# One scan-attention and two-MLP kernel on one Trainium2 core: squared products copied out of PSUM by one ScalarE operation, the last attention outputs in the state's bank, and fp32 key-value products in the first attention

## The chip, the cores and the metric

The kernel runs on 1 core of one Trainium2 chip. The metric is the device time of one execution in microseconds (us). The kernel before takes 816.45 us (median of 3 runs, 816.13 to 817.19). PE is TensorE, DVE is VectorE, ACT is ScalarE, POOL is GpSimd, and SP is the engine whose queue issues every DMA here.

## What is computed

There are three stages for each of four batch entries (S = 768 positions, H = 8 heads, D = 48, C = H*D = 384).

```python
# 1. attention with a decaying complex state, position by position
S_re, S_im = ar * S_re - ai * S_im + outer(k[t], v[t]), ar * S_im + ai * S_re
y[t] = q[t] @ S_re
# 2. token mixing, then channel mixing (256 and 1536 hidden)
u = x + (relu(x.T @ w_tok1) @ w_tok2).T
x = u + relu(u @ w_ch1) @ w_ch2
# 3. a gated layer with squared relu (1024 hidden) on a mix of each row and the row before
out = sigmoid(xr @ w_r) * (relu(xk @ w_k) ** 2 @ w_v)
```

## The kernel before, in words

**Attention.** The scan is done in 6 blocks of 128 positions (J = 0 to 5). Decays and angles are first turned into logs and summed (the words S, L, A, R, C, D of `SEQ0` and `SEQ1`), and then one step per block follows (T0 to T7, since later parts of a block's work come one or two steps after its first). `ORD0` and `ORD1` (L35, L36) give the order of the parts within a step by hand; the digit behind a name says how many blocks back it works. The parts are: `b` scales q and k by their decays (DVE); `q` and `k` turn them into complex pairs `q2`, `k2` in fp32 (DVE, tile `Wc`) and take the upper fp16 part (ACT); `e` takes the lower fp16 part (DVE); each of these four fp16 parts is transposed by a DMA (`transposed`, L546). `w` splits v into the fp16 parts `vh` (ACT) and `vl` (DVE). `f` makes the scores (PE, 12 products per group of four heads) and `m` masks them (DVE). `u` (L624) makes k x v for the state: 24 fp16 products of 128 x 48, three for each head, plus two with an identity matrix that add the state carried over. `v` takes the state out of its PSUM bank as two fp16 parts (ACT, then DVE). `h` (L668) makes the outputs y in PSUM from the transposed q, the state and the masked scores, and `i` takes them out as `xh` (ACT) and `xl` (DVE). `l` loads q, k and v two blocks on.

In the first attention (b = 0) nothing of another batch entry runs beside it. There the scores times v are fp32 products, with a scaled fp32 copy `v32` of v that the part `a` (L558) makes at the end of a step. Its banks alternate between two pairs. In it, PE's, ACT's and DVE's instructions of the steps are chained in the order of `ORD0` (L334 to L346 and L479 to L483), and every load and transpose is chained in SP's queue (`queue`, L524). For blocks below 3, `keep_busy` (L485) adds 6 idle products (fillers, tile `h1b`, L489) behind each part that issues products; they have the lowest priority. In the other attentions (b = 1 to 3) there is one bank "u" for the state and one bank "y" for the outputs.

**Dense layers.** `dense(b)` runs beside `attention(b + 1)`; the main loop (L960 to L974) advances the two in proportion to costs written by hand. `two_layers` (L796) goes through items (t, f). For each item it makes 9 products into one of two PSUM banks (`ps_d`, tile `ps`), and `evac1` takes the result out as two fp16 parts in the tile `g`. The second layer's 9 products on these parts come `LAG` = 2 items later. For the gated layer (wk1 and wv2, 16 items for each batch entry) `wk1_out` (L907) does three ACT operations and one DVE operation on the bank:

```python
ACT(ps, ps, ACTF.Relu)                                   # L908
ACT(ps, ps, ACTF.Square, scale=...)                      # L909
ACT(part[:, 0], ps, ACTF.Copy)                           # L910
last_ev[:] = [TT(part[:, 1], ps, part[:, 0], op=SUB)]    # L911
```

Weights arrive as pairs of 32-bit words and are unpacked on DVE (L266 to L268), rounded to the upper fp16 part (DVE L271 or ACT L273) and to the lower one (DVE L277); they load into two buffers `wst`. A small ACT operation `seen` (L186) collects sums of squares for a validity test at the end, one column of the tile `low` for each call. The program is ordered before it runs: each instruction has a priority, and the order on each engine comes from these priorities and from the chains.

Of the kernel before, what the change touches and what calls it, by code (L numbers as in the profile page):

```python
# [8 lines left out]
F32 = mybir.dt.float32  # L9
# [4 lines left out]
ACTF = mybir.ActivationFunctionType  # L14
# [3 lines left out]
B, H, S, D = 4, 8, 768, 48  # L18
C = H * D
NJ = S // 128  # L20
# [11 lines left out]
SEQ0 = "S0 L0 S1 L1 B1 A0 R0 A1 R1 C0 C3 C1 C4 C2 D0 C5 D1 T0 T1 T2 T3 T4 T5 T6 T7"  # L32
SEQ1 = "S0 S1 L0 L1 A0 R0 A1 R1 C0 C1 C2 D0 C3 C4 C5 D1 T0 T1 T2 T3 T4 T5 T6 T7"

ORD0 = "f01 f11 b0 w0 q0 k0 e0 i2 v1 u0 m01 m11 h01 h11 x2 a0 l0"  # L35
ORD1 = "b0 w0 u1 v1 q0 f01 m01 g01 f11 k0 h01 m11 g11 e0 h11 i1"  # L36

BEHIND = "fh"
# [17 lines left out]
X_S, U_S, XK_S, XR_S, SQ_S = 6, 5, 5, 3, 14  # L56
T1_S, T2_S, C1_S, C2_S, WK_S, WV_S, WR_S = 6, 5, 6, 7, 6, 6, 3
# [11 lines left out]
ROUND_L = 1.5 * 2.0 ** (11 + L_S + 1)  # L69


STATS = {"wp": 8, "wm": 8, "wbits": 1, "wsum": 26, "xsum": 48, "osum": 24, "low": 36, "re": 2, "rmin": 6}
NSTAT = sum(STATS.values()) + STATS["wp"] + STATS["wm"]
LOW_MIN = 48.0
UNIT = 2.0 ** L_S
# [25 lines left out]
def split_path(  # L101
# [10 lines left out]
    MUL, ADD, SUB, MAX, MIN = ALU.mult, ALU.add, ALU.subtract, ALU.max, ALU.min  # L112
# [205 lines left out]
    def hd(x):  # L318
        return x.rearrange("p (h d) -> p h d", h=H)
# [5 lines left out]
    last_ev = []  # L325
    tables = [None, [], []]

    def attention(b):
# [75 lines left out]
        def bank(tag, J, shape):  # L404
            if b == 0 and J % 2:
                return ps_a.tile(shape, F32, tag={"u": "a0", "y": "a1"}[tag], name=tag)
            return ps_1.tile(shape, F32, tag=tag, name=tag)
# [73 lines left out]
        def MM(**k):  # L481
            last_mm[:] = [nc.tensor.matmul(**k)]  # L482
            behind(last_mm, ahead if b == 0 else passed)  # L483
# [73 lines left out]

        def s_a(J):  # L558
            d = st[J]
            d["v32"] = hd(V32[J % 2])  # L560
            ACT(d["v32"], d["v"], ACTF.Copy, scale=col_c[:, 2:3])
            if J + 1 < NJ:
                turn(J + 1)
            return 0.0

        def s_b(J):
# [9 lines left out]
                load(J + 1, "q")  # L576
            return 1.33

        def s_w(J):
            d = st[J]  # L580
            ACT(d["vh"], d["v"], ACTF.Copy, scale=col_c[:, 2:3])
            STT(d["vl"], d["v"], col_c[:, 2:3], d["vh"], op0=MUL, op1=SUB)
            if J == 0:
                seen(d["vh"][:, :, 0:LOW_N // H])
            if b > 0:
                load(J + 1, "v")
            return 0.5
# [36 lines left out]
        def s_u(J):  # L624

            if J == NJ - 1:
                return 0.0
            d = st[J]
            U = bank("u", J, [128, H, D])
            Uf = d["U"] = U.rearrange("p h d -> p (h d)")  # L630
            with tc.high_priority(offset=P_PE):
                def carried():
                    for i in range(2 if J > 0 else 0):
                        MM(out=Uf, lhsT=id1[0:96], rhs=T16[0:96, 2 * i + J % 2], start=b > 0 and i == 0, stop=b == 0 and i == 1)

                if b > 0:
                    carried()
                for h in range(H):
                    for n_, (a_, b_) in enumerate(THREE):
                        MM(out=U[:, h], lhsT=sets[J % 2]["k" + a_][:, h], rhs=d["v" + b_][:, h],  # L640
                                         start=(J == 0 or b == 0) and h == 0 and n_ == 0, stop=h == H - 1 and n_ == 2 and (b > 0 or J == 0))
                if b == 0:
                    carried()
            return 0.0
# [23 lines left out]
        def s_h(J, g):  # L668
            d = st[J]
            if g == 0:  # L670
                d["y"] = bank("y", J, [128, H, D])
            y = d["y"]
            with tc.high_priority(offset=P_PE):
                for h in range(4 * g, 4 * g + 4):
                    if J > 0:
                        th, tl = hd(T16[0:96, J % 2]), hd(T16[0:96, 2 + J % 2])
                        for n_, (a_, b_) in enumerate((("h", th), ("h", tl), ("l", th))):
                            MM(out=y[:, h], lhsT=Tr[J % 2]["q" + a_][0:96, h], rhs=b_[:, h], start=n_ == 0, stop=False)
                    if b == 0:
                        MM(out=y[:, h], lhsT=d["m", g][:, h % 4], rhs=d["v32"][:, h], start=J == 0, stop=True)  # L680
                    for n_, (m_, v_) in enumerate(((0, "vh"), (0, "vl"), (1, "vh")) if b > 0 else ()):
                        MM(out=y[:, h], lhsT=M16[g][m_][:, h % 4], rhs=d[v_][:, h], start=J == 0 and n_ == 0, stop=n_ == 2)
            return 0.0
# [22 lines left out]
            return lambda J: fn(J, *a)  # L706

        cq, ck = late(s_c, "q"), late(s_c, "k")
        fns = {"a": s_a, "x": s_x, "l": s_l, "b": s_b, "w": s_w, "q": cq, "k": ck, "e": s_e, "i": s_i, "u": s_u, "v": s_v}
        fns.update({nm + str(g): late(fn, g) for nm, fn in (("f", s_f), ("g", s_g), ("h", s_h), ("m", s_m)) for g in range(2)})  # L710
        order = [(x[0], fns[x[:-1]], int(x[-1])) for x in (ORD0 if b == 0 else ORD1).split()]

# [38 lines left out]
    def dense(b):  # L751
# [44 lines left out]
        def two_layers(nf, first, second, evac1, evac2, at=None):  # L796

            items = [(t, f) for t in range(2) for f in range(nf)]
            parts, acc = {}, {}
            for n_ in range(len(items) + LAG):  # L800
                if n_ < len(items):
                    t, f = items[n_]
                    ps = ps_d.tile([128, N], F32, tag="d", name="ps")
                    first(t, f, ps)
                    part = gring.tile([128, 2, N], F16, tag="g", name="g")
                    with tc.high_priority(offset=P_EV):
                        evac1(ps, part)
                        if n_ == 0:
                            seen(part[:, 0, 0:LOW_N])
                    parts[t, f] = part  # L810
                    yield 9 * MM
                    if at and n_ in at:
                        yield from at[n_]()
                if n_ >= LAG:
                    t, f = items[n_ - LAG]
                    if f == 0:
                        acc[t] = [ps_a.tile([128, N], F32, tag=f"a{i}", name=f"a{i}") for i in range(3)]
                    part = parts.pop((t, f))
                    for i in range(3):
                        second(t, f, i, part, acc[t][i], f == 0, f == nf - 1)  # L820
                        if f == nf - 1:
                            evac2(t, i, acc[t][i])
                    yield 9 * MM
# [8 lines left out]
            for c in range(3):  # L832
                mm3(ps, [w[:, c, 128 * f:128 * f + 128] for w in wc1], [x[:, c] for x in u[t]], c == 0, c == 2)

        def ch1_out(ps, part):
            ACT(part[:, 0], ps, ACTF.Relu)  # L836
            last_ev[:] = [STT(part[:, 1], ps, 0.0, part[:, 0], op0=MAX, op1=SUB)]  # L837

# [65 lines left out]
            for c in range(3):  # L904
                mm3(ps, [w[:, c, 128 * f:128 * f + 128] for w in wk], [x[:, c] for x in xk[t]], c == 0, c == 2)

        def wk1_out(ps, part):  # L907
            ACT(ps, ps, ACTF.Relu)  # L908
            ACT(ps, ps, ACTF.Square, scale=2.0 ** (SQ_S // 2 - XK_S - WK_S))  # L909
            ACT(part[:, 0], ps, ACTF.Copy)  # L910
            last_ev[:] = [TT(part[:, 1], ps, part[:, 0], op=SUB)]  # L911

        def wv2(t, f, jj, part, ps, start, stop):
            need(("v", f))
# [331 lines left out]
```

## Time and profile before

| what | value |
|---|---|
| median of the runs | 816.45 us |
| the profiled execution | 818.82 us, of which the span is 817.0 us |
| mean granted TensorE clock | 0.974 of full |
| PE busy | 741.3 us (91%) |
| DVE busy | 581.8 us (71%) |
| ACT busy | 522.6 us (64%) |

The profiled execution lies 2.37 us above the median, and its span is 1.82 us shorter than its own time. The first attention takes the span's first 115 us or so. dense(0) to dense(3) begin at about 116, 320, 500 and 671 us. In the rows below, a time in square brackets is the idle time of the engine before that row and what ended it.

### The profile page before, as it was taken

The page shows a single profiled execution, that of the slowest core. Times are in us where ns is not written, and L with a number is a line of the kernel's source. Part 1 is how long each engine was busy: PE and PEld are TensorE (multiplying, and loading weights), DVE is VectorE, ACT ScalarE, POOL GpSimd, SP SyncE. Part 2 cuts the span into 40 slices and gives each one's busy share as a digit, 9 for nine tenths or more (in the row PEclk, how much of TensorE's full clock was granted, in tenths as well). Part 3 has the DMA queues.
Part 4 walks back from the last instruction along what each step waited for, and adds up shares of the span by engine and source line. Part 5 has one row for each costly group of instructions (what it writes and reads, how often), then busy time and mean ns, then how long its engine had stood idle before and what let it go on. Part 6 is the DMA issues. An engine that isn't in the chain of part 4 may idle for free.

```text
span 817.0 us, 15178 instructions
## 1 busy us (share of the span) xinstructions
PE 741.3 (91%) x6107; PEld 471.4 (58%) x6107; DVE 581.8 (71%) x1016; ACT 522.6 (64%) x988; POOL 21.3 (3%) x53
## 2 busy tenths in 40 slices
PE   0968878999989889999998989999999999999996
PEld 0557845455555455555665656566666666666553
DVE  3998978999998738887768448777776454484822
ACT  7884559777588779674568778566576532142752
POOL 3000000001010000000000000000000000010000
PEclk9987989999999999999999989999999999999998
DMA  8249983444673851052336331141333342868200
GB/s 273 78 118 205 195 264 136 130 154 118 176 137 82 194 120 49 20 122 55 62 63 120 91 85 49 46 104 26 63 62 63 81 134 79 268 198 261 103 30 33
DMA packets 137949, 94.92 MB, mean 116 GB/s; under 512 B 104592, under 2 KB 120208, under 8 KB 137872
## 3 DMA queue, kind: packets, MB, share of 16 engines
q1 hardware_dynamic: 137872, 93.88, 45.2%
q8 instruction: 50, 0.82, 0.4%
q14 instruction: 27, 0.22, 0.1%
HBM read 63.97 MB, written 4.72 MB: 84 GB/s over the span
## 4 chain that ended last, share of the span: by engine, by line
PE 47%; DVE 21%; ACT 15%; DMA 12%; issue 3%; SPq 1%; DVEq 0%; ACTq 0%
PE ps L741 22%; PE a L741 14%; PE y L482 4%; DVE X L337 4%; ACT X L337 3%; DMA X<-by_time_a_re_dram 3%; PE u L482 3%; DMA wst<-in_moe_w_k_dram 2%; DVE Wc L337 2%; PE sp L482 2%; ACT tmp L875 2%; DMA Rc<-qh 1%; DVE g L837 1%; DMA wst<-in_moe_w_v_dram 1%; DVE ql L337 1%
## 5 line engine op out<-in xcount | busy, mean ns | idle before, releaser
L741 PEld LDWEIGHTS <-wc 128*128 128x128 f16 x1728 | 166.7, 98 | 116.9 <-issue 9.5
L741 PE MATMUL ps<-uh,wc 128*128 128x384 f16 x576 | 156.3, 326 | 2.1 <-DVE ul L793 1.2
L741 PE MATMUL a<-g,wc 128*128 128x384 f16 x864 | 157.9, 326 | 0.0
L741 PE MATMUL ps<-xkh,wk 128*128 128x384 f16 x384 | 106.4, 331 | 3.5 <-DVE g L911 3.3
L741 PE MATMUL a<-wv,g 128*128 128x384 f16 x576 | 106.9, 328 | 2.5 <-ACT g L910 2.5
L836 ACT ACTIVATE g<-ps 128x384 f16<-128x384 f32 x96 | 46.4, 484 | 78.0 <-PE ps L741 76.6
L741 PE MATMUL ps<-ul,wc 128*128 128x384 f16 x288 | 93.8, 326 | 0.0
L482 PEld LDWEIGHTS <-Rc 96*128 96x128 f16 (+1 forms) x1416 | 69.8, 100 | 34.4 <-issue 13.9
L837 DVE SCALAR_TENSOR_TENSOR g<-ps,g 128x384 f16<-128x384 f32 x96 | 52.9, 554 | 37.4 <-ACT g L836 37.2
L741 PEld LDWEIGHTS <-wk 128*128 128x128 f16 x576 | 55.6, 99 | 39.9 <-issue 6.4
L741 PEld LDWEIGHTS <-g 128*128 128x128 f16 x576 | 54.9, 98 | 37.4 <-ACT g L910 3.0
L741 PE MATMUL ps<-xkl,wk 128*128 128x384 f16 x192 | 63.5, 331 | 0.0
L911 DVE TENSOR_TENSOR g<-ps,g 128x384 f16<-128x384 f32 x64 | 35.3, 553 | 35.1 <-ACT g L910 34.9
L482 PE MATMUL y<-CH,Rc 96*128 96x48 f16 (+1 forms) x912 | 42.9, 186 | 9.7 <-DVE xl L337 5.2
L908 ACT ACTIVATE ps<-ps 128x384 f32<-128x384 f32 x64 | 30.4, 476 | 30.9 <-PE ps L741 29.5
L337 DVE TENSOR_TENSOR m<-sp,tri 128x512 f32<-128x512 f32 x48 | 32.6, 685 | 20.5 <-PE sp L482 19.7
L482 PE MATMUL sp<-Rc 96*128 96x128 f16 x504 | 39.2, 225 | 8.6 <-DVE m L337 3.3
L337 DVE TENSOR_TENSOR Wc<-cs,X 128x768 f32<-128x768 f32 x48 | 44.8, 951 | 0.2
L337 ACT ACTIVATE X<-X 128x1152 f32<-128x1152 f32 x32 | 37.1, 1159 | 11.5 <-DMA X<-by_time_a_re_dram 9.6
L337 ACT ACTIVATE X<-X,col_c 128x1152 f32<-128x1152 f32 x32 | 40.0, 1252 | 1.2 <-DVE X L337 0.4
L482 PE MATMUL u<-CH,kh 128*128 128x48 f16 x320 | 36.2, 188 | 3.4 <-ACT kh L337 3.4
L337 DVE TENSOR_TENSOR Rc<-m,Rc 128x512 f16<-128x512 f32 x36 | 24.8, 689 | 18.6 <-ACT Rc L337 18.6
(212 smaller groups left out, 1377.9 us busy)
## 6 DMA issues: line engine op xcount, KB each, us to landing
wst<-in_moe_w_ch_dram SPq DMA_DIRECT2D x24, 768.0 KB, 4.4
CH<-in_qk_dram SPq DMA_DIRECT2D x18, 384.0 KB, 3.2
wst<-in_moe_w_tok_dram SPq DMA_DIRECT2D x8, 768.0 KB, 5.0
wst<-in_moe_w_k_dram SPq DMA_DIRECT2D x8, 768.0 KB, 4.5
wst<-in_moe_w_v_dram SPq DMA_DIRECT2D x8, 768.0 KB, 4.6
X<-by_time_a_re_dram SPq DMA_DIRECT2D x8, 576.0 KB, 4.8
X<-by_time_a_im_dram SPq DMA_DIRECT2D x8, 576.0 KB, 6.9
CH<-by_time_v_dram SPq DMA_DIRECT2D x24, 192.0 KB, 2.7
```

The source lines that it names most:

```text
L337: ins = fn(*a, **k)
L482: last_mm[:] = [nc.tensor.matmul(**k)]
L741: ins = [nc.tensor.matmul(out=ps, lhsT=lh[a_], rhs=rh[b_], start=start and n_ == 0, stop=stop and n_ == 2) for n_, (a_, b_) in enumerate(( ...
L836: ACT(part[:, 0], ps, ACTF.Relu)
L837: last_ev[:] = [STT(part[:, 1], ps, 0.0, part[:, 0], op0=MAX, op1=SUB)]
L875: ACT(w[:, 0:N], z[:, 0:N], ACTF.Copy, scale=o[:, c:c + 1])
L908: ACT(ps, ps, ACTF.Relu)
L911: last_ev[:] = [TT(part[:, 1], ps, part[:, 0], op=SUB)]
```

## The change

- `ORD0` loses the part `w` and gains the part `p` behind `k`. `s_p` makes the fp32 copy `v32`, which `s_a` made before. In the first attention the fp16 parts `vh` and `vl` are no longer made, and one call of `seen` goes (`low` has 35 columns).
- In the first attention `s_u` makes k x v as 8 fp32 products (96 x 48 outputs, from `k2` in the tile `Wc` and from `v32`) in place of 24 fp16 ones. The two products that add the carried state stay.
- In the attentions 1 to 3 the outputs of the last block (J = 5) go to the bank "u" and not to the bank "y".
- `wk1_out`: the relu goes from PSUM to an fp32 SBUF tile `r` by one ACT operation. In the first batch entry (b = 0) a square and a copy on ACT and the subtraction on DVE follow, all from SBUF. In the others ACT squares `r` into the upper part, DVE squares `r` in place and DVE subtracts: two operations on ACT and two on DVE in place of three and one. `r` has two slots, by f even or odd (those of the tiles `h1h` and `h1l`).

```diff
-ORD0 = "f01 f11 b0 w0 q0 k0 e0 i2 v1 u0 m01 m11 h01 h11 x2 a0 l0"
+ORD0 = "f01 f11 b0 q0 k0 p0 e0 i2 v1 u0 m01 m11 h01 h11 x2 a0 l0"
...
         def s_a(J):
             d = st[J]
-            d["v32"] = hd(V32[J % 2])
-            ACT(d["v32"], d["v"], ACTF.Copy, scale=col_c[:, 2:3])
             if J + 1 < NJ:
                 turn(J + 1)
             return 0.0
...
+        def s_p(J):
+            d = st[J]
+            d["v32"] = hd(V32[J % 2])
+            ACT(d["v32"], d["v"], ACTF.Copy, scale=col_c[:, 2:3])
+            return 0.0
+
         def s_w(J):
+            if b == 0:
+                return 0.0
...
             with tc.high_priority(offset=P_PE):
+                n = 96 if b == 0 else 128
+
                 def carried():
                     for i in range(2 if J > 0 else 0):
-                        MM(out=Uf, lhsT=id1[0:96], rhs=T16[0:96, 2 * i + J % 2], start=b > 0 and i == 0, stop=b == 0 and i == 1)
+                        MM(out=Uf[0:n], lhsT=id1[0:96, 0:n], rhs=T16[0:96, 2 * i + J % 2], start=b > 0 and i == 0, stop=b == 0 and i == 1)
 
                 if b > 0:
                     carried()
-                for h in range(H):
+                for h in range(H if b == 0 else 0):
+                    MM(out=U[0:96, h], lhsT=W[:, 1, h].rearrange("p c d -> p (c d)"), rhs=d["v32"][:, h], start=h == 0, stop=h == H - 1 and J == 0)
+                for h in range(H if b > 0 else 0):
                     for n_, (a_, b_) in enumerate(THREE):
                         MM(out=U[:, h], lhsT=sets[J % 2]["k" + a_][:, h], rhs=d["v" + b_][:, h],
-                                         start=(J == 0 or b == 0) and h == 0 and n_ == 0, stop=h == H - 1 and n_ == 2 and (b > 0 or J == 0))
+                                         start=J == 0 and h == 0 and n_ == 0, stop=h == H - 1 and n_ == 2)
...
             if g == 0:
-                d["y"] = bank("y", J, [128, H, D])
+                d["y"] = bank("u" if b > 0 and J == NJ - 1 else "y", J, [128, H, D])
...
-        def wk1_out(ps, part):
-            ACT(ps, ps, ACTF.Relu)
-            ACT(ps, ps, ACTF.Square, scale=2.0 ** (SQ_S // 2 - XK_S - WK_S))
-            ACT(part[:, 0], ps, ACTF.Copy)
-            last_ev[:] = [TT(part[:, 1], ps, part[:, 0], op=SUB)]
+        def wk1_out(ps, part, f):
+            r = one.tile([128, C], F32, tag=f"h1{'hl'[f % 2]}", name="r")
+            ACT(r, ps, ACTF.Relu, scale=2.0 ** (SQ_S // 2 - XK_S - WK_S))
+            if b == 0:
+                ACT(r, r, ACTF.Square)
+                ACT(part[:, 0], r, ACTF.Copy)
+            else:
+                ACT(part[:, 0], r, ACTF.Square)
+                TT(r, r, r, op=MUL)
+            last_ev[:] = [TT(part[:, 1], r, part[:, 0], op=SUB)]
```

## Rows read from the trace of the kernel before

**Rows 1.** The page, part 1: engine, busy us (share of the span), instructions.

```profile
PE 741.3 (91%) x6107; PEld 471.4 (58%) x6107; DVE 581.8 (71%) x1016; ACT 522.6 (64%) x988; POOL 21.3 (3%) x53
```

**Rows 2.** Stretches of 20 us: length, busy PE, PEld, DVE, ACT, POOL, clock, DMA, GB/s.

```profile
80.00:100.00 20.00, 17.91 (x291) 16.16 (x289) 19.02 (x30) 13.28 (x25) 0.00 (x0) 1.00 0.98 177
...
420.00:440.00 20.00, 19.20 (x192) 12.31 (x191) 18.31 (x40) 16.83 (x40) 0.00 (x0) 1.00 0.38 81
```

**Rows 3.** Waits of PE from 110 us on: us in total, times, longest us.

```profile
PE y L482 <- DVE xl L337: 5.2, 2, 2.8
...
PE ps L741 <- DVE g L911: 3.3, 4, 2.6
...
PE h1a L741 <- DVE xl L337: 3.1, 1, 3.1
PE a L741 <- ACT g L910: 2.5, 2, 1.3
```

**Rows 4.** Timeline of DVE, start of the first attention's steps: start us, us, operation.

```profile
50.21 0.61 DVE L337 SCALAR_TENSOR_TENSOR CH<-CH,col_c 128x384 f16<-128x384 f32 x1
50.74 1.82 DVE L337 TENSOR_TENSOR Wc<-cs,X 128x768 f32<-128x768 f32 x2
```

**Rows 5.** Timeline of PE, steps 2 and 3 of the first attention.

```profile
74.44 0.92 PE L489 MATMUL h1b<-tri 128*128 128x128 f16 x7
75.15 0.25 PE L482 MATMUL u<-CH,kl 128*128 128x48 f16 x1
...
76.06 0.81 PE L482 MATMUL u<-CH,id 96*128 96x384 f16 x2
...
77.43 0.61 PE L482 MATMUL y<-v32l,m 128*128 128x48 f32 x2
77.84 0.32 PE L482 MATMUL y<-CH,Rc 96*128 96x48 f16 x3
...
79.06 0.40 PE L482 MATMUL y<-v32l,m 128*128 128x48 f32 x2
79.30 0.24 PE L482 MATMUL y<-CH,Rc 96*128 96x48 f16 x3
...
83.30 1.17 PE L489 MATMUL h1b<-tri 128*128 128x128 f16 x18
...
84.86 0.48 PE L482 MATMUL u<-CH,id 96*128 96x384 f16 x2
```

**Rows 6.** Timeline of SP's queue: the transposes of block 3 begin.

```profile
80.22 1.24 SPq L547 DMA_TRANSPOSE Rc<-qh  x1
```

**Rows 7.** Waits of SP's queue, 48 to 118 us.

```profile
SPq L547 <- PE y L482: 3.0, 1, 3.0
```

**Rows 8.** Timeline of PE: three of the waits, in dense(0) and dense(1).

```profile
306.93 0.28 PE L482 MATMUL y<-CH,Rc 96*128 96x48 f16 x3 [2.39 <-DVE xl L337]
...
447.96 0.32 PE L741 MATMUL ps<-xkh,wk 128*128 128x384 f16 x1 [2.56 <-DVE g L911]
...
485.19 0.20 PE L482 MATMUL y<-CH,Rc 96*128 96x48 f16 x1 [2.77 <-DVE xl L337]
```

**Rows 9.** Timeline of ACT ahead of the wait at 447.96.

```profile
444.42 1.16 ACT L337 ACTIVATE wide<-X 128x1152 f32<-128x1152 f32 x1 [1.64 <-DMA X<-by_time_a_im_dram]
...
446.84 0.47 ACT L910 ACTIVATE g<-ps 128x384 f16<-128x384 f32 x1
```

**Rows 10.** Timeline of DVE: the first attention's end, and beside the two y waits.

```profile
113.93 0.56 DVE L266 TENSOR_SCALAR wf<-wst 128x768 int32<-128x768 int32 x1 [3.77 <-DMA wst<-in_moe_w_ch_dram]
...
307.18 0.69 DVE L337 TENSOR_TENSOR Rc<-m,Rc 128x512 f16<-128x512 f32 x1 [0.30 <-ACT Rc L337]
...
485.06 0.68 DVE L337 TENSOR_TENSOR Rc<-m,Rc 128x512 f16<-128x512 f32 x1
```

**Rows 11.** Groups by shape: count, busy us, mean ns, idle before and its releasers.

```profile
L911 DVE TENSOR_TENSOR g<-ps,g 128x384 f16<-128x384 f32 x64 | 35.3, 553 | 35.1 <-ACT g L910 34.9
L910 ACT ACTIVATE g<-ps 128x384 f16<-128x384 f32 x64 | 30.9, 483 | 0.9
```

**Rows 12.** The chain that ended last, gated stage of dense(3): start us, us, what.

```profile
770.61 1.46 PE a L741 x9
```

More of the change, by code (lines that the diff above doesn't have):

```diff
@@ L69 @@
 ROUND_L = 1.5 * 2.0 ** (11 + L_S + 1)
-STATS = {"wp": 8, "wm": 8, "wbits": 1, "wsum": 26, "xsum": 48, "osum": 24, "low": 36, "re": 2, "rmin": 6}
+STATS = {"wp": 8, "wm": 8, "wbits": 1, "wsum": 26, "xsum": 48, "osum": 24, "low": 35, "re": 2, "rmin": 6}
 NSTAT = sum(STATS.values()) + STATS["wp"] + STATS["wm"]
@@ L708, in attention @@
         cq, ck = late(s_c, "q"), late(s_c, "k")
-        fns = {"a": s_a, "x": s_x, "l": s_l, "b": s_b, "w": s_w, "q": cq, "k": ck, "e": s_e, "i": s_i, "u": s_u, "v": s_v}
+        fns = {"a": s_a, "x": s_x, "l": s_l, "p": s_p, "b": s_b, "w": s_w, "q": cq, "k": ck, "e": s_e, "i": s_i, "u": s_u, "v": s_v}
         fns.update({nm + str(g): late(fn, g) for nm, fn in (("f", s_f), ("g", s_g), ("h", s_h), ("m", s_m)) for g in range(2)})
@@ L806, in two_layers @@
                     with tc.high_priority(offset=P_EV):
-                        evac1(ps, part)
+                        evac1(ps, part, f)
                         if n_ == 0:
@@ L833, in ch1, with ch1_out @@
                 mm3(ps, [w[:, c, 128 * f:128 * f + 128] for w in wc1], [x[:, c] for x in u[t]], c == 0, c == 2)
-        def ch1_out(ps, part):
+        def ch1_out(ps, part, f):
             ACT(part[:, 0], ps, ACTF.Relu)
```

## The prediction, made before the changed kernel was run

> **What bounds the kernel now.** I read the page's engine totals first: PE is busy 91% of 817.0 us, DVE 71% [rows 1]. So after the first attention, where dense products fill PE, a saved ACT or DVE operation is worth only what it takes out of a wait of PE. The second view is therefore PE's waits from 110 us on. The reader is to see how small they are: those that name parts which the change touches come to 3.3 us (the next products wait for a bank that L911 still reads), 2.5 us (the second layer waits for L910), and 5.2 us (outputs y wait for the last copy `xl` out of their bank) [rows 3]. That is 11.0 us, 1.3% of the run, and the most that edits there can give by taking waits away. The third view is the table of 20 us stretches, for the first attention: from 80 to 100 us DVE is busy 19.0 of 20 us, the DMA engines 98%, and PE 17.9 us with fillers among them [rows 2]. There three resources are close to full, so work taken off one gives little if another gets more.
>
> **The fp16 parts of v leave the first attention.** This takes 6 copies off ACT and 6 `vl` off DVE. In the first step `vl` starts at 50.21 and `Wc` follows at 50.74, so each is worth 0.53 us of DVE's queue [rows 4]. The first step starts the row of transposes, so I count its 0.53 us as a gain of 0.5. The others stand where DMA engines and PE are also full [rows 2]; I count them at nothing. Bounds: 0 and 6 x 0.53 = 3.2 us gained. The earlier `v32` costs nothing: it is the same operation on ACT, which has 6.7 us free in those 20 [rows 2]. Behind it now queue `xh` of block J-2 and the state copy of `v`; both are asked for by PE only after `u`. One validity operation fewer is under 0.5 us on ACT, in the same cover.
>
> **k x v in fp32.** The trace has no fp32 product with 96 weight columns; the nearest rows are the scores times v, 128 x 48. In their steady sequence the fp32 pair starts at 79.06 and what follows at 79.30, so a head takes 0.24 us; at 77.43, where PE had just been waiting and its clock was low, the same pair took until 77.84, 0.41 us [rows 5]. Block 2: 8 x 0.41 = 3.3 us against 0.9 (75.15 to 76.06) for most of the fp16 products; the 7 fillers between take 0.7 (74.44 to 75.15) and stand there because the third product of a head waited for `kl`, which fp32 products no longer need [rows 5]. If they go elsewhere the step gets 3.3 - 1.6 = 1.7 us longer; if they stay, 2.4. By the 0.24 row it is 1.9 - 1.6 = 0.3. I take 1.5, near the low-clock row, since the same low clock rules there. Block 3: 8 x 0.24 = 1.9 us against 1.6 (83.30 to 84.86, of which 18 fillers take 1.2) [rows 5]: 0.3 longer, or 1.5 if the fillers stay, I take 0.4. Blocks 0 and 1 end in PE's waits for transposes, and block 4's extra us lies ahead of transposes that queue for the DMA engines: nothing, at most 1.0.
> Why is PE's time here on the path? SP's queue waits 3.0 us for PE's outputs y, once [rows 7]: the transposed q of block 3 goes into the buffer that the outputs of block 1 still read, and so starts only at 80.22 [rows 6]. From there the queue runs nearly without a gap to the loads of the next batch entry. What PE loses ahead of 80.22 is lost to the first attention's end. Sum of this part: +1.9 (bounds +0.3 and +4.9).
> The Trainium skill ("TensorE: Matmul & The Clock Gate", LDWEIGHTS) says that a weight load is timed by its columns and not by its rows. By that rule 96 columns would load in three quarters of the time, and as an estimate this part would be about +0.5.
>
> **Squared products leave PSUM by one operation.** 64 times the bank comes free after the relu and not after three ACT operations and a DVE one. The wait at 447.96 shows the gain [rows 8]: between relu and L910 ACT stood behind the next attention's squares, which waited 1.64 us for their DMA and ran until 445.6; L910 came at 446.84 [rows 9]. With the bank free, PE goes on with one item (9 products, 1.46 us [rows 12]), and then asks for this part. I take 2.0 of the 2.56 there and 0.7 for the other three of that kind: -2.7 of 3.3 [rows 3]. The 2.5 us of the second layer [rows 3] are two waits at a stage's start; one ACT operation fewer (483 ns [rows 11]) stands before the upper part: 2 x 0.5 = -1.0. Bounds of both: 0 and 5.8 gained.
> The price: 48 times DVE gets one more operation, about as long as L911 (553 ns [rows 11]): 26.5 us. Mostly DVE's idle time covers it, but at the start of a gated stage DVE has none (18.3 of 20 us from 420 to 440 [rows 2]): some five items of three such stages, 15 x 0.55 = 8.3 us, if all of it fell on the path. PE needs a part only two items later, so I take +1.0 (bounds 0 and 8.3). What is late if this cover goes: the masks `m` of the attention beside it. The ACT operations saved (48 x 0.48 = 23 us) I count at nothing beyond the above.
>
> **The last outputs in the state's bank.** PE waits 2.39 us at 306.93 and 2.77 at 485.19 for `xl` of block 4 [rows 8]. With the other bank they no longer wait for it. But what comes next is late as well: the lower parts of the masked scores `Rc`, which DVE makes at 307.18 to 307.87 and at 485.06 to 485.74 [rows 10]. What can move ahead are the products with the state and the rest of the scores. I take -0.4 and -1.2, together -1.6 (bounds 0 and -5.2). The state's bank is free in time: the outputs read the copies made from it in any case.
>
> **The sum.** -0.5 + 1.9 - 2.7 - 1.0 + 1.0 - 1.6 = -2.9 us. On the profiled execution's 818.82 (span 817.0) that is 815.9; the median lies 2.37 lower, so I forecast 816.45 - 2.9 = 813.6 us.
>
> **The rivals.**
> *DVE's queue (slower).* `r` has two slots, and the relu of item f + 2 waits until DVE has subtracted item f. Where DVE is full, ACT, which works in order, stands at that relu, and behind it the attention's copies. It decides from the point where DVE is later than two items (4 x 1.46 = 5.8 us with both layers [rows 12]) less the operations themselves (about 2.1). For it: DVE is 92% busy at a stage's start [rows 2]. Against: such a stretch is short. Price: all 8.3 us in place of 1.0, 816.45 - 2.9 + 7.3 = 820.9.
> *The next wait takes the place of the one removed (no change).* The waits of PE in the gated stages and at y end where the next attention's data land (the DMA in [rows 9]), and `Rc` ends just behind `xl` [rows 10]. If half of the 5.3 us comes back: 816.45 - 2.9 + 2.65 = 816.2.
> *The end of the first attention comes out in another order (faster).* DVE's `xl` of block 5 stands behind `wf`, which waits 3.77 us for weights [rows 10], and PE waits 3.1 us for that `xl` [rows 3]. The order there is the priorities' and not a chain's, and shorter steps could put `xl` first: 816.45 - 2.9 - 3.1 = 810.5. Against: nothing in the change says so.
> *Narrow weights (faster).* 96 columns load faster than 128. Then block 2 costs 0.75 x 3.3 - 1.6 = 0.9 and block 3 0.75 x 1.9 - 1.6, nothing: +0.9 in place of +1.9, 812.6. No weight load in the trace has fewer columns than 128. The skill's rule above is this rival's.
>
> **How the numbers follow.** Forecast 0.38, DVE's queue 0.22, next wait 0.20, other order 0.12, narrow weights 0.08. 0.2% is 1.6 us, about what a measurement of this kernel can tell from no change. Of the forecast 0.32 lies below 814.8, since its terms are each unsure by some us, and 0.03 on either further side; the next-wait case is no change, with bounds that leave nothing of it beyond. Faster 0.32 + 0.12 + 0.08 = 0.52; same 0.20 + 0.03 = 0.23; slower 0.22 + 0.03 = 0.25. The range reaches from the other order, with a little of the bounds (3.2 us of `vl`), to the full price of DVE: 809.0 to 821.0. The likeliest case alone would be 811.5 to 816.0.
>
> **What would show it.** Right: in the first attention u has 16 fp32 records in a block, and SP waits longer than 3.0 us for y at the transposes of block 3, which start near 81. No wait of PE of over 0.5 us ends at L911's successor; the y waits end at `Rc` and are 1 to 2 us. DVE's total is about 20 us higher (+26.5, less 6 x 0.6 and PSUM reads), ACT's about 25 lower. Wrong: a relu that waits for DVE (the rival), a first attention that ends before 114 us (then fp32 cost nothing or the order changed), or y waits of the old length.

## The result, and the profile after

The kernel after takes 811.41 us (median of 15 runs, 805.67 to 815.58), the kernel before, beside it, 818.41 us (15 runs, 814.80 to 821.07). The ratio is 0.9917, with a 95% interval of 0.9893 to 0.9940: faster by 6.8 us, where 2.9 were forecast, and just under the 811.5 at which the likeliest case ended. Single executions of the kernel after differ by 10 us. The profiled one is the fastest (805.67 us, span 803.9), so its stages are read for where time went and the ratios for how much.

The page of after, part 1 (answers to [rows 1]):

```profile
PE 741.2 (92%) x6067; PEld 473.4 (59%) x6067; DVE 601.4 (75%) x1058; ACT 501.8 (62%) x932; POOL 20.9 (3%) x53
```

PE's work is the same. DVE has 19.6 us more and ACT 20.8 us less (about 20 and 25 were forecast). Stretches of after (answer to [rows 2]; the first is in dense(0)):

```profile
80.00:100.00 20.00, 19.46 (x263) 17.44 (x262) 18.79 (x28) 9.29 (x15) 0.00 (x0) 0.95 1.11 180
...
160.00:180.00 20.00, 15.77 (x73) 7.70 (x72) 17.09 (x26) 12.55 (x21) 0.00 (x0) 0.83 0.65 172
...
420.00:440.00 20.00, 19.09 (x194) 12.21 (x191) 19.86 (x40) 16.95 (x30) 0.00 (x0) 1.00 0.54 123
```

Waits of PE in after, from 106 us on (answer to [rows 3]):

```profile
PE u L482 <- ACT Rc L337: 4.7, 2, 2.7
PE sp L482 <- DVE m L337: 4.4, 6, 2.0
PE ps L751 <- DVE g L847: 3.1, 4, 1.4
...
PE ps L751 <- ACT wc L273: 2.4, 1, 2.4
```

Of the two kinds of waits on the squared products [rows 3], 3.3 and 2.5 us, 0.5 us is left. The wait for `xl` at y is gone by name, but outputs y, now in the bank "u", wait 4.7 us for the upper part of `Rc`. New is a wait of 2.4 us for a weight (`wc`) in dense(0). The squared products' groups (answer to [rows 11]):

```profile
L926 DVE TENSOR_TENSOR g<-r,g 128x384 f16<-128x384 f32 x64 | 35.5, 554 | 1.7 <-ACT g L922 0.3
L919 ACT ACTIVATE r<-ps 128x384 f32<-128x384 f32 x64 | 30.8, 482 | 37.1 <-PE ps L751 36.9
L925 DVE TENSOR_TENSOR r<-r 128x384 f32<-128x384 f32 x48 | 26.6, 553 | 24.3 <-ACT g L924 24.1
```

The relu (L919) waits for PE alone, never for DVE.

Where the time went is seen in stages. A stage begins with the first copy of `h1` in dense(b), or with the first relu of the gated layer, on ACT's timeline. Lengths in us, one profiled execution each ("squares" is the third part of the change alone, e12 below):

| stage | before | squares | after |
|---|---|---|---|
| first attention, to the first copy of `h1` | 115.6 | 111.9 | 106.8 |
| dense(0) up to the gated layer | 118.5 | 117.9 | 128.5 |
| gated layer, dense(0) | 86.1 | 83.9 | 77.8 |
| dense(1) up to the gated layer | 103.8 | 103.7 | 102.9 |
| gated layer, dense(1) | 75.7 | 72.9 | 72.2 |
| dense(2) up to the gated layer | 103.2 | 103.7 | 103.8 |
| gated layer, dense(2) | 68.3 | 67.4 | 67.5 |
| dense(3) up to the gated layer | 87.2 | 86.8 | 86.8 |
| gated layer, dense(3), to the end | 58.6 | 57.9 | 57.6 |

In this table the first attention is 8.8 us shorter, but the gated layer of dense(0) begins 1.2 us later than before (106.8 + 128.5 = 235.3 against 234.1). The gain in hand at dense(1) is 7.1 us, against 6.5 with the squares alone. (The squares change nothing in the first attention, not even an order there; its 3.7 us in this execution, 1.7 in another, are the difference of two executions. The six kernels profiled with the old first attention took 111.9 to 115.6 us there.)

### The profile page after: what moved, and what is told of

It reads as the page before. It is cut to its first block, busy times and chain, and to the rows that moved or that the text cites. A ratio compares the mean times of both kernels' runs of the same rounds, so it can differ in the third digit from the quotient of the medians.

```text
span 803.9 us, 15080 instructions
## 1 busy us (share of the span) xinstructions
PE 741.2 (92%) x6067; PEld 473.4 (59%) x6067; DVE 601.4 (75%) x1058; ACT 501.8 (62%) x932; POOL 20.9 (3%) x53
## 4 chain that ended last, share of the span: by engine, by line
PE 51%; DVE 23%; ACT 13%; DMA 9%; issue 3%; SPq 1%; DVEq 0%; ACTq 0%
PE ps L751 21%; PE a L751 15%; PE y L482 4%; PE u L482 4%; ACT X L337 3%; DVE X L337 3%; PE sp L482 3%; DMA X<-by_time_a_re_dram 2%; DMA wst<-in_moe_w_k_dram 2%; DVE tmp L886 2%; DVE g L847 1%; DVE Wc L337 1%; ACT L337 1%; DVE ql L337 1%; DVE tmp L868 1%
## 5 line engine op out<-in xcount | busy, mean ns | idle before, releaser
L751 PE MATMUL ps<-xkh,wk 128*128 128x384 f16 x384 | 105.0, 328 | 0.0
L482 PEld LDWEIGHTS <-Rc 96*128 96x128 f16 (+1 forms) x1416 | 67.9, 99 | 32.4 <-DVE Rc L337 8.0
L919 ACT ACTIVATE r<-ps 128x384 f32<-128x384 f32 x64 | 30.8, 482 | 37.1 <-PE ps L751 36.9
L925 DVE TENSOR_TENSOR r<-r 128x384 f32<-128x384 f32 x48 | 26.6, 553 | 24.3 <-ACT g L924 24.1
L482 PE MATMUL y<-CH,Rc 96*128 96x48 f16 (+1 forms) x768 | 35.8, 184 | 3.6 <-DVE Rc L337 2.1
L337 ACT ACTIVATE qh<-Wc 128x768 f16<-128x768 f32 x24 | 20.1, 839 | 26.9 <-DVE Wc L337 19.2
```

Of the source, the lines that this page charges most:

```text
L337: ins = fn(*a, **k)
L751: ins = [nc.tensor.matmul(out=ps, lhsT=lh[a_], rhs=rh[b_], start=start and n_ == 0, stop=stop and n_ == 2) for n_, (a_, b_) in enumerate(( ...
L919: ACT(r, ps, ACTF.Relu, scale=2.0 ** (SQ_S // 2 - XK_S - WK_S))
L925: TT(r, r, r, op=MUL)
```

## The experiments

**The parts alone, and all again** (measured side by side). Each of the first three has the hunks of one part of the change: e1 those of the first attention, e2 that of the bank, e3 those of `wk1_out`; e4 is the kernel after once more. One line of each:

```diff
-ORD0 = "f01 f11 b0 w0 q0 k0 e0 i2 v1 u0 m01 m11 h01 h11 x2 a0 l0"
+ORD0 = "f01 f11 b0 q0 k0 p0 e0 i2 v1 u0 m01 m11 h01 h11 x2 a0 l0"
```

> The kernel before with the fp32 k x v products and the part p alone (no fp16 parts of v in the first attention). My theory now, from the two traces: the first attention ends about 8 us earlier because a weight load of 768 KB no longer stands in SP's queue between the loads of block 2 and the transposes of block 1, and one weight load fewer runs inside it; the first dense layer's channel stage then takes about 10 us longer for want of weights. So the first h1 copy comes at about 107 us (116 before), the gated stage of dense(0) begins at 232 to 237 us (234 before), and the whole moves by -1 to -4 us. The prediction's term for this part alone (+1.4 us, 817.9 on 816.45) would have the first h1 copy at 116 to 119 us.

```diff
-                d["y"] = bank("y", J, [128, H, D])
+                d["y"] = bank("u" if b > 0 and J == NJ - 1 else "y", J, [128, H, D])
```

> The kernel before with the last outputs in the state's bank alone. Prediction's term: -1.6 us; PE's waits of 2.4 and 2.8 us for xl become waits of 1 to 2 us for Rc. Rival (the next wait takes the place of the one removed): within 0.8 us of before, same total wait ahead of the last outputs. A gain of over 3 us would mean that the order around the end of an attention changed as well.

```diff
-            ACT(ps, ps, ACTF.Relu)
+            ACT(r, ps, ACTF.Relu, scale=2.0 ** (SQ_S // 2 - XK_S - WK_S))
```

> The kernel before with the new wk1_out alone (relu into SBUF, DVE squares in the entries 1 to 3). Prediction's terms: -2.7 -1.0 +1.0 = -2.7 us; the waits of PE that end at L911 (3.3 us) and at L910 (2.5 us) go to under 1.5 us together, DVE is 20 us busier, ACT 20 us less. Rival (DVE's queue): 0 to +7 us, with relus that wait for DVE.

> The changed kernel once more, beside the three single parts on the same chip. If the parts add up, its difference to before is the sum of the three within 2 us; measured so far -0.83% (-5 to -8 us). If it gains 3 us or more beyond the sum, two parts need each other. Its single executions should again spread over some 10 us (805.7 to 815.6 so far, before 814.8 to 821.1).

Measured against before (817.44 us): fp32 products 813.58 us, ratio 0.9919 (0.9889 to 0.9950); bank 817.69 us, 1.0006 (0.9984 to 1.0028); squared products 807.17 us, 0.9889 (0.9864 to 0.9913); all 808.13 us, 0.9889 (0.9864 to 0.9914). So the squared products alone give what the whole change gives, the bank gives nothing, and the fp32 part gives 6.6 us alone and nothing that can be measured beside the squares. The parts do not add up: -15.2 us by these ratios, -9.1 for all. (The ratios follow the means more than the medians: e1's medians differ by 3.9 us only, since four of its nine runs lie at 806 to 808 us and five at 813 to 817. Its profiled run is the slowest, with the first copy of `h1` at 115.3 us and not the expected 107; the section on the clock shows why.) PE's waits in the run with the bank alone show why it is worth nothing:

```profile
PE u L482 <- ACT Rc L337: 4.7, 3, 2.5
```

The outputs used to wait 5.2 us for `xl`; now they wait 4.7 for the very next thing, `Rc`.

**The weight load alone.** In after, the weight load that stood ahead of block 1's transposes stands behind block 2's. Here the kernel before gets that order, and nothing else.

```diff
-pri.enter_context(tc.high_priority(offset=P_W[phase[0]]))
+pri.enter_context(tc.high_priority(offset=-600 if i==3 else P_W[phase[0]]))
```

> The kernel before with one edit: the unpacking of the fourth piece of weights has a lower priority, so that the weight load that stood ahead of block 1's transposes stands behind block 2's, as in the kernel after, and one later load falls behind the first attention. Products, copies and banks are as before. Theory 'place of the load': the shorter first attention of the kernel after comes from this place, so the first copy of h1 comes before 110 us here too, the transposed kh of block 1 no longer takes over 4 us, and the median is 3 to 5 us under the kernel before (about 813). Rival 'fp32 products and vl': the gain comes from what no longer runs on ACT, DVE and PE, so the first copy of h1 stays at 114 to 116 us and the median within 1.6 us of before.

Measured: 814.92 us against 815.88, ratio 0.9985 (0.9957 to 1.0012). The first copy of `h1` came at 110.5 us, 5 us earlier than in before and 1.4 us earlier than in any of the six kernels above, and `kh` of block 1 took 2.35 us; but at dense(1) only 1.7 us were left (318.5 against 320.2). Each theory is half right: the place of the load shortens the first attention, but the run's gain cannot be told from noise.

**vl made again.** The kernel of e1 with `vh` and `vl` made as before, read by nothing. With them the weight work falls back into its old places.

```diff
-ORD0 = "f01 f11 b0 q0 k0 p0 e0 i2 v1 u0 m01 m11 h01 h11 x2 a0 l0"
+ORD0 = "f01 f11 b0 w0 q0 k0 p0 e0 i2 v1 u0 m01 m11 h01 h11 x2 a0 l0"
...
         def s_w(J):
-            if b == 0:
-                return 0.0
```

> The kernel with the fp32 products alone (ratio 0.9919), in which the fp16 parts vh and vl of the first attention are made again, though nothing reads them; the order of the step has them where the kernel before had them, and the weight load is ahead of block 1's transposes again. Theory 'DVE and its queue': what PE does in fp32 gains nothing by itself, the gain comes from six vl (0.6 us each) and the weight work that no longer stand in DVE's order, so the ratio goes back to 0.997 to 1.003 and the first copy of h1 to 113 to 117 us. Rival 'products': the gain comes from PE no longer waiting for kl and vl, ratio 0.990 to 0.994 and the first copy of h1 at 107 to 110 us.

Measured: 818.66 us against 817.85, ratio 1.0000 (0.9971 to 1.0029); first copy of `h1` at 114.5 us. The fp32 products by themselves neither gain nor cost anything that shows; the gain of e1 came from `vh` and `vl` leaving, and what moved with them. SP's queue, first of e10, then of after:

```profile
59.80 0.38 SPq L255 DMA_DIRECT2D wst<-in_moe_w_ch_dram  x1
60.27 1.49 SPq L547 DMA_TRANSPOSE Rc<-qh  x1
61.86 4.73 SPq L547 DMA_TRANSPOSE kt<-kh  x1
```

```profile
59.25 1.24 SPq L547 DMA_TRANSPOSE Rc<-qh  x1
60.59 1.81 SPq L547 DMA_TRANSPOSE kt<-kh  x1
...
74.17 0.42 SPq L255 DMA_DIRECT2D wst<-in_moe_w_ch_dram  x1
75.89 1.24 SPq L547 DMA_TRANSPOSE Rc<-qh  x1
```

And DVE's timeline at the start of step 1, before, then after:

```profile
55.74 0.95 DVE L277 SCALAR_TENSOR_TENSOR wt<-wst,wt 128x768 f16<-128x768 f32 x1
...
56.62 0.61 DVE L337 SCALAR_TENSOR_TENSOR CH<-CH,col_c 128x384 f16<-128x384 f32 x1
57.15 1.82 DVE L337 TENSOR_TENSOR Wc<-cs,X 128x768 f32<-128x768 f32 x2
```

```profile
54.51 1.15 DVE L337 SCALAR_TENSOR_TENSOR X<-qk,col_c,X 128x384 f32<-128x384 f32 x2
55.57 1.93 DVE L337 TENSOR_TENSOR Wc<-cs,X 128x768 f32<-128x768 f32 x2
```

Before, a weight operation (L277) and `vl` stood ahead of block 1's `Wc`; after, nothing does, and `Wc` is 1.58 us earlier. The weight load that `kh` ran beside (4.73 us with it ahead, 1.81 without) goes into the buffer that L277 reads, so it can be issued only behind L277.

**The squared products taken apart.** Two things changed at once: the bank comes free after the relu, and ACT does two operations and not three. e8 has the first without the second, e9 the second without the first, and e12 is both again, with six more runs.

The edit of e8, in the new form:

```diff
-            if b == 0:
+            if True:
                 ACT(r, r, ACTF.Square)
                 ACT(part[:, 0], r, ACTF.Copy)
```

> The kernel before with the squared products' way out alone, and that in the form of the first batch entry for all four: relu out of PSUM, square and copy on ACT from SBUF, subtraction on DVE; no square on DVE. Against the squared products alone as changed (ratio 0.9889, about 807 us). Theory 'release of the bank': the gain comes from the bank coming free after the relu, and DVE's 48 squares cost 1 us at most, so the ratio is 0.987 to 0.991 here. Rival 'DVE's queue': the squares on DVE cost up to 8.3 us, so this kernel is 3 to 8 us faster (ratio 0.979 to 0.985). Rival 'ACT's share': the gain comes from ACT doing two operations and not three, so that half or more of it is lost here (ratio 0.994 or above).

The edit of e9, in the old form:

```diff
-            ACT(part[:, 0], ps, ACTF.Copy)
+            if b == 0:
+                ACT(part[:, 0], ps, ACTF.Copy)
+            else:
+                TS(part[:, 0], ps, 1.0, None, op0=MUL)
             last_ev[:] = [TT(part[:, 1], ps, part[:, 0], op=SUB)]
```

> The kernel before with one edit: in the gated stages of batch entries 1 to 3 the copy to the upper part is made by DVE and not by ACT. So there are two operations on ACT and two on DVE, as in the kernel after, but the bank is held to the last of them, as in the kernel before. With the run without DVE's square (bank free after the relu, three operations on ACT, ratio 0.994) and the squared products as changed (both, 0.9889) this is the fourth corner. Theory 'each has its share': ACT's shorter work is worth about what that run did not get, so the ratio is 0.993 to 0.996. Rival 'only together': with the bank held to the end by an engine that is full at a stage's start nothing is gained, ratio 0.998 to 1.004, and the wait of the next products for the bank is as long as before (2.5 us) or longer. Rival 'all of it is ACT': ratio 0.991 or lower.

> The squared products' way out alone, as in the kernel after, a second time and with more runs (the first ratio, 0.9889, stands on 6 runs). Theory 'this part is the whole of the gain': ratio 0.987 to 0.991 again, so that the two other parts add nothing to it, and the corners of the square are 1, 0.994 (bank free early), 0.995 (ACT's work halved) and this. Rival 'the first six runs were low': ratio 0.992 to 0.996, so that bank and ACT's share do not add up and the fp32 part has a share in the gain of the whole change.

Measured: bank free early 0.9940 (0.9915 to 0.9964), ACT's work cut 0.9951 (0.9924 to 0.9979), both 0.9893 (0.9871 to 0.9916). The two halves, 0.60% and 0.49%, add up to the whole, 1.07%: as "each has its share" expects, ACT's shorter work and the early release are both worth something. (e8's own theory, that the release is all of it, missed: it asked for 0.987 to 0.991.) e9 and the whole hold 48 more DVE operations each; no run shows their cost by itself. The groups of the subtraction in e9, to be held against L911 in [rows 11], and of the copy that DVE now makes ahead of it:

```profile
L914 DVE TENSOR_TENSOR g<-ps,g 128x384 f16<-128x384 f32 x64 | 35.3, 552 | 5.2 <-ACT g L911 4.5
L913 DVE TENSOR_SCALAR g<-ps 128x384 f16<-128x384 f32 x48 | 26.5, 552 | 25.3 <-ACT ps L909 25.2
```

Before, DVE waited 34.9 us in total for ACT's copy ahead of the subtraction. In e9 4.5 us are left there, but 25.2 stand ahead of DVE's copy, for ACT's square: most of this wait has moved and not gone, so its length is not what e9 gained. One part still goes through four operations in turn; what is shorter is ACT's share of it, 0.95 us and not 1.43 (two or three operations of 0.47 to 0.48). ACT then waits more for PE ahead of the relu (L908), 36.1 us against 29.5. And with the bank held to the last operation, as before, the 2.56 us wait of [rows 8] is gone all the same (PE's waits of e9):

```profile
PE a L741 <- DVE g L913: 2.3, 2, 1.2
...
PE ps L741 <- DVE g L914: 1.3, 4, 0.6
```

What held PE up at 447.96 was ACT's late copy; either cure works there.

**All without the bank.** After one execution of each, the bank seemed to cost 2 us in the gated layer of dense(1) beside the other parts.

```diff
-d["y"] = bank("u" if b > 0 and J == NJ - 1 else "y", J, [128, H, D])
+d["y"] = bank("y", J, [128, H, D])
```

> The kernel after with the last outputs in bank y again (fp32 products and squared products as changed). Theory 'the bank costs': from the gated stage of dense(1) to dense(2) the kernel with all parts took 72.7 us where the squared products alone took 70.1, with the clock down in the one and not in the other; without the bank that stage takes 70 to 71 us and the median is 2 us or so under that of all parts (about 806). Rival 'the bank is nothing': that stage stays at 72 to 73 us and the median is that of all parts within 1.5 us.

Measured: 810.58 us against 815.88, ratio 0.9915 (0.9882 to 0.9948), with that stage at 71.2 us. It can't be told from all parts (0.9917 and 0.9889); what it seemed to cost was the difference of two executions. The 12 runs lie in two groups, 803.9 to 805.7 (5) and 810.0 to 814.1 (7).

**The clock in the first attention.** Two executions with the same instructions there, a stretch of PE each: e1's profiled one, then after's.

```profile
66.00:86.00 20.00, 20.00 (x150) 18.92 (x148) 10.48 (x17) 7.32 (x16) 0.00 (x0) 0.50 0.76 169
```

```profile
66.00:86.00 20.00, 20.00 (x277) 18.99 (x276) 17.86 (x28) 11.77 (x23) 0.00 (x0) 0.97 1.13 234
```

PE is busy throughout in both, with a granted clock of 0.50 (1.2 GHz) in the one and 0.97 (nearly all at 2.4 GHz) in the other. At the lower clock PE becomes the bound: SP's queue in e1 waits 13.1 us for the outputs y, in three waits,

```profile
SPq L547 <- PE y L482: 13.1, 3, 8.5
```

the transposes of block 3 start at 82.94 and not 75.89, and the first copy of `h1` comes at 115.3 us, as before. Did this make the two groups of runs? The next kernel fills PE's idle time ahead of it.

```diff
 def step(s):
     at[0] = s
+    if b == 0 and s == 0:
+        keep_busy(40)
...
-        keep_busy(N_FILL)
+        keep_busy(36 if s == 0 else N_FILL)
```

> The kernel after with 40 idle products ahead of the first step and 36 in place of 6 behind each part of that step, nothing else. Theory 'clock': executions of the kernel after differ by 10 us because TensorE's granted clock comes back at about 67 us in some and at about 86 us in others, after PE's idle stretches between 51 and 61 us; with these stretches filled the clock is near 1.0 from 54 to 70 us, the first copy of h1 comes at 107 us or earlier, and all runs lie within 5 us, with a median of 804 to 807. Rival 'fillers in the way': PE executes them in order ahead of the scores, the scores of block 0 come 1 to 2 us later, and the median is that of the kernel after or up to 2 us above, with the same spread of 10 us.

Measured: 812.45 us against 815.88, ratio 0.9930 (0.9893 to 0.9967), 804.85 to 817.59 us. The profiled execution's stretch shows what the fillers did:

```profile
54.00:66.00 12.00, 10.07 (x139) 9.11 (x136) 12.00 (x18) 7.89 (x14) 0.00 (x0) 1.00 1.15 201
```

The clock stayed at 1.00 there (0.50 in after), the first copy of `h1` came at 105.0 us, and yet this execution took 812.0 us of span: it lost its lead in dense(0) (dense(1) began at 316.0, in after at 313.1), 2.1 us more in dense(1) up to the gated layer, and 2.5 in one wait of PE where the gated layer of dense(3) begins. So the clock theory fell: in the profiled execution the fillers held the clock, and the spread of the runs is as wide as without them. The rival's median and spread came, but not for its reason, since nothing in the first attention is late. The clock explains e1's execution; what parts the runs of the other kernels stays open.

**Weights earlier.** If dense(0) gives the first attention's gain back because weights are late, they might be unpacked sooner.

```diff
-P_W = (-300, 100)
+P_W = (-100, 100)
```

> The fp32 products and the squared products (without the bank; ratio 0.9915), with one number changed: the weight unpacking in the first attention has a priority offset of -100 and not -300, so that four weight loads that came behind the first attention come within it. Theory 'given back in dense(0)': what the first attention gained came back in dense(0) as waits of PE for weights (2.4 and 1.6 us, and a channel stage 10 us longer), so with the weights earlier the first copy of h1 comes 2 to 4 us later, the first one of dense(1) 2 to 4 us earlier, and the median is 1 to 4 us under that without this edit. Rival 'DVE is the bound in both places': the weight work costs the first attention what dense(0) gets, the first copy of h1 comes 6 us or more later, and the median is the same or up to 4 us above.

Measured (from the kernel without the bank, 0.9915): 819.81 us against 817.85, ratio 1.0020 (0.9993 to 1.0046). dense(0) no longer waits for weights, its part up to the gated layer took 121.3 us, where the kernel without the bank took 128.2; but the first copy of `h1` came at 127.5 us. PE's and ACT's timelines show the new wait:

```profile
97.40 2.80 PE L482 MATMUL u<-v32h,Wc 128*96 128x48 f32 x16 [5.67 <-ACT v32h L337]
```

```profile
89.25 0.91 ACT L273 ACTIVATE wc<-wst 128x768 f16<-128x768 f32 x1 [4.90 <-DVE wst L268]
90.12 0.84 ACT L337 ACTIVATE qh<-Wc 128x768 f16<-128x768 f32 x1
96.00 0.84 ACT L337 ACTIVATE kh<-Wc 128x768 f16<-128x768 f32 x1 [5.03 <-DVE Wc L337]
```

ACT, whose operations come in the program's order, stands at the weight's rounding for 4.90 us, then for block 4's `Wc` on the same DVE, and PE behind both. Weight work costs the first attention more than dense(0) gets: the rival's side, and by twice its size (0.0105 of 818 us, 8.6 us, against up to 4).

No version beat both kernels clearly: the squared products alone (0.9889 and 0.9893) are as fast as anything run here, with 6 runs each within 5 us.

## Why the prediction was right, and where its steps failed

The sign and the range held; the forecast of 813.6 us stood for a ratio of 0.9965, and 0.9917 was measured. But the terms were far from what the runs show:

| step | forecast, us | alone, us |
|---|---|---|
| `vl` off DVE | -0.5 | -6.6 with the fp32 products |
| k x v in fp32 | +1.9 | 0 (e10, within 2.4) |
| squared products | -2.7 | -9.1 and -8.8 |
| last outputs in bank "u" | -1.6 | +0.5 (within 1.8) |

The column "alone" is the ratio less 1, times the median of before beside it.

**vl.** The step that failed is "The others stand where DMA engines and PE are also full [rows 2]; I count them at nothing", and with it the bound of 3.2 us. It priced the operation and not its place: an operation gone from the head of a chain also let the weight work that stood around it move (DVE above), and with that a load in SP's queue. None of this is in the diff. It then came back in dense(0): PE is busy 15.77 us from 160 to 180, at a clock of 0.83, where the kernel before had 20.00 at 1.00:

```profile
160.00:180.00 20.00, 20.00 (x88) 9.49 (x88) 18.39 (x33) 14.55 (x28) 0.20 (x2) 1.00 0.38 123
```

The prediction followed the first attention only to its end. That what is saved at the head of that chain is saved at its end was right; its size, and that dense(0) gives it back, was missed. That the first attention ended at 106.8 us, before 114, is one of the prediction's own signs of being wrong ("then fp32 cost nothing or the order changed").

**Other order**, a faster rival, came about, and paid little. Before, PE waited 3.1 us for `xl` of block 5, which stood on DVE behind `wf` [rows 3, 10]. In after this `xl` starts at 104.88 us, the next `wf` only at 109.81, and the wait is gone: some 3 of the 8.8 us. The prediction's "nothing in the change says so" overlooked that the weight work moves: in e5, where only that was moved, the order is the same (108.50 and 114.64), and in e10, where it fell back, `wf` is ahead again (112.35, then `xl` at 112.83). The price of 3.1 us was not earned as priced: e5 kept nothing that shows.

**fp32.** The prices were bounded by 128-column rows (0.41 and 0.24 us a head). Start to next start, e1 at the lower clock and the repeated kernel after (e4) at the higher:

```profile
61.48 2.74 PE L482 MATMUL u<-v32l,Wc 128*96 128x48 f32 x16
64.02 0.52 PE L482 MATMUL u<-CH,id 96*96 96x384 f16 x1
```

```profile
72.03 1.51 PE L482 MATMUL u<-v32h,Wc 128*96 128x48 f32 x16
73.38 0.49 PE L482 MATMUL u<-CH,id 96*96 96x384 f16 x2
```

That is 2.54 and 1.35 us for 8 heads, 0.32 and 0.17 a head: the rival's narrow weights, 0.75 of the wider rows (2.5 and 1.4), was right about the price. The Trainium skill ("TensorE: Matmul & The Clock Gate", LDWEIGHTS) has the time of a weight load go by its columns; these rows agree (0.32 against 0.41 and 0.17 against 0.24 us). The prediction's estimate of +0.5 beside that rule does not follow from its own sum for this rival, +0.9. The whole term, +1.9, lies within e10's interval of 2.4 us, so no run rules it out. The claim that PE ahead of block 3's transposes is on the path held only at the lower clock: SP waited 13.1 us for y in e1's execution, but 2.4 us, in three waits, in after's, where the transposes began at 75.89. So "near 81" and "longer than 3.0" were wrong for the profiled execution.

**Squared products.** The direction was right and the waits named (447.96, and those for L910) are gone. The step that failed is "The ACT operations saved (48 x 0.48 = 23 us) I count at nothing beyond the above": e8 and e9 give ACT's shorter work nearly half of the gain. [Rows 11] pointed there: with DVE idle 34.9 us for ACT's L910, ACT's three operations stood ahead of each part's last one. A second miss is that waits were priced by their length. In the gated layer of dense(1) the first run of the squares was 5.6 us shorter than before (70.1 against 75.7), twice the wait that went, and its clock there was 1.00 where before had 0.72 (before, then the first run, where the same wait for `xl` ends at 477 us and not at 485):

```profile
480.00:490.00 10.00, 7.23 (x60) 4.81 (x59) 4.69 (x6) 9.26 (x14) 0.00 (x0) 0.72 0.01 2
470.00:480.00 10.00, 7.74 (x103) 5.49 (x102) 7.04 (x11) 9.69 (x13) 0.00 (x0) 1.00 0.05 16
```

The second run, e12, fell to 0.78 and 0.88 there (470 to 490 us) and was 2.8 us shorter, so some of this differs from one execution to the next.

**DVE's queue**, the slower rival, fell: DVE was busy 19.86 of 20 us from 420 to 440, as feared, but no relu waited for it, and the kernel with its squares (e12) beats the one without (e8), which has ACT's third operation in their place. The price of 1.0 us was not measured by itself.

**The bank.** "With the other bank they no longer wait for it" was true and worth nothing: the rival "the next wait takes the place" is what happened, for this part, and by ACT's `Rc`, a step ahead of the DVE one that was named. The longest wait there is still 2.7 us, which by the prediction's own test makes this step wrong.

**The sum** came near by luck. Alone, the first attention's part gave 8.0 us more than forecast (-6.6 against +1.4), the squared products 6.4 or 6.1 more, and the bank 2.1 less: -15.2 us in all, where -2.9 were forecast. But the parts do not add, and the whole gave -6.8 and -9.1. At dense(1) it is 7.1 us ahead of before and the squares alone 4.7 (e3) to 6.5 (e12). The overlap is seen in the gated layer of dense(0): the squares alone took it from 86.1 to 83.9 us, but e1, without them, took 77.3 and after, with them, 77.8. So what that layer takes back of dense(0)'s loss comes with the first attention's part; why was not taken apart. That the shorter first attention is spent waiting for weights is shown in part: PE's waits for `wc` in dense(0) up to the gated layer come to 5.5 of the 10.0 us lost there, and e11, which has none of them, lost less.

## What to carry to other kernels

An operation removed from a full, ordered queue also moves what the scheduler had put around it, transfers included: read the new order of every queue before pricing the operation, and follow the gain into the next stage, which may be waiting for what was moved out. When several engines make a part in turn, the idle time of the last operation's group names the engine that it waits for, which the share of busy time does not; it gives no price, since most of it moved in e9 and 0.49% was gained all the same. Run each part alone and its halves crossed, since parts that fill the same idle time do not add.

## What was not expected of the hardware

With the same instructions in the first attention, PE busy for 20.00 of 20 us had a granted clock of 0.50 in one execution and 0.97 in another (66 to 86 us, above). In both PE had waited 2.30 us just ahead of block 0's products (they start at 53.06 us in e1 and at 53.71 in after), and the clock was 0.50 by 58 us. From 62 us on PE was busy without a gap in both; the clock came back between 66 and 68 us in after and between 86 and 88 in e1. Why so much later is not shown. A transpose by DMA of 1.81 us (after) took 4.73 us in e10, with a weight load issued 2.06 us ahead of it (61.86 - 59.80), and 2.35 in e5, where only the load's place differs from before (4.83).
